# Second parts of the fixed weights on VectorE, and weight sums pipelined over three buffers, in a fused attention, routing and MLP kernel

## The chip, the cores and the metric

One core of a Trainium2 chip. The metric is the device time of one execution in microseconds (us), the median over runs.

## The reference, cut to what matters

```python
# q, k, v: (8, 8, 576, 64); k and v pooled by 8 along the sequence
attn = softmax(scale * q @ k_pool.T) @ v_pool
x = attn.transpose(0, 2, 1, 3).reshape(4608, 512)
# routing: all (token, expert) logits in falling order; a token goes to the first
# of the 8 experts that still has room (capacity 576)
for e in range(8):
    h = np.maximum(x[assigned == e] @ w1[e], 0.0)      # 512 -> 1024
    out[assigned == e] = h @ w2[e]                     # 1024 -> 512
h = np.maximum(out @ w_in, 0.0)                        # 512 -> 2048, fixed weights
result = (h * h) @ w_out                               # 2048 -> 512, fixed weights
```

All inputs and the result are f32.

## The kernel before, in words

After the attention the 4608 tokens are routed, one expert after another, in rounds: a round makes a table `gep` on VectorE (L868), sums it on TensorE (L889), turns the sums on VectorE into counts (`rmd` to `rcd`, L892 to L898), sums again on TensorE (L903) and sets the next bounds on VectorE (`rck` to `rhold`, L905 to L854). Each expert's 576 tokens are then gathered and taken through four layers: the expert's two, the fixed in-layer and the fixed last layer. The text counts them 1 to 4 (or "last").

To keep f32 precision with f16 matmuls, weights and activations are split into two f16 parts, a first part (the rounded value) and a second (the remainder), and each product takes three passes (first by first, first by second, second by first). Expert 0 runs the fixed in-layer plainly (L1266, from `wi`); experts 1 to 7 use a form with seven products of mixed weights (L1403), for which sums and differences of quarters of `w_in` are made once and kept in DRAM as `mixed_weights`. The last layer is L1460, from `wo`.

The program is written out by a Python recorder. The layers of the experts run in the foreground; beside them stand tasks (Python generators: `conv_rest`, `tokens`, `feed`, `routes`, `split_first`, `split_fixed`, `mix_first`) that the recorder advances by estimated engine times: each `yield` names an estimated time from which the task goes on, and `bg.add` gives the order and the engines that it is charged to. What a task records lands on the engines' queues there and then, and every engine works through its queue in order. Small matmuls of the routing so land between the matmuls of the layers.

The tasks that the change touches:

- `split_first` splits `w_in`, eight chunks of 128x1024, in place in `wi`. The first part goes to a side buffer, the second is the chunk minus its first part (`low`, L695), on GpSimd in two halves, into a `gfm` tile of the pool `r_p`; `place` (L699, L700) then copies both into `wi` by DMAs from SP.
- `split_fixed` splits `w_out` into `wo`. The first four chunks go by ACT and GpSimd, the last four, once expert 0's second layer is recorded, by ACT (L779), VectorE (L781) and two DMAs (L782, L783) from two `gfm` tiles.
- `mix_first` first copies the plain quarters to `mixed_weights` (L730, 24 DMAs), then makes the mixed ones in sixteen pieces: load (L740), four sums on GpSimd (L749 to L752), first part on ACT (L755), second on GpSimd (L756), store (L759). Two buffers for the input; one for the parts, in the third slot of `mixb`.
- the gather of the next expert's tokens splits each tile of 128 tokens into `h`, a `gfm` tile, and turns it by a transposing DMA (L1205 to L1208).

The pool `r_p` has two buffers for each name, so a third `gfm` tile waits until the first has been read, here by its DMA. Of `conv_rest`, which decodes the raw weights, the prediction names L661 (VectorE), and of the weight splits of the experts L1106.

## Time and profile before

| what | value |
|---|---|
| median of 3 runs | 1396.54 us (1395.21 to 1402.73) |
| the profiled execution's own time | 1394.52 us |
| its span in the profile | 1392.8 us |
| mean granted TensorE clock | 0.963 |
| PE busy | 1293.1 us (93%) |
| VectorE (DVE) busy | 882.6 us (63%) |
| ScalarE (ACT) busy | 646.7 us (46%) |
| GpSimd (POOL) busy | 443.1 us (32%) |

A busy share is a mean over stages with different limits. PE works nearly all the time, so the places where it stands, and the stretches at a lower clock, are what other engines can take from or give to the time. In the rows below `x24` is the number of instructions in a group, a bracket at the end tells how long the engine stood idle before it and what ended that, and `SPq` is SP issuing DMAs.

### The profile page before, as it was taken

What the parts mean: (1) busy time and instruction counts of PE and PEld (TensorE: products, weight loads), DVE (VectorE), ACT (ScalarE), POOL (GpSimd) and SP (SyncE); (2) the same over time, 40 slices, a digit from 0 to 9 for tenths busy, and PEclk for the clock granted to TensorE, in tenths of its full rate; (3) what the DMA queues carried; (4) which work ended last, traced back from release to release, by engine and by line L of the source; (5) the groups of instructions that cost most, each with busy time, mean ns of one, the idle gap of its engine ahead of it and who ended that gap; (6) DMA issues with size and microseconds to landing.
All of it is one profiled execution on the core that took longest, in us unless ns stands there. A gap on an engine that the chain in (4) does not pass through costs nothing.

```text
span 1392.8 us, 25459 instructions
## 1 busy us (share of the span) xinstructions
PE 1293.1 (93%) x9925; PEld 921.3 (66%) x9925; DVE 882.6 (63%) x2179; ACT 646.7 (46%) x1257; POOL 443.1 (32%) x457
## 2 busy tenths in 40 slices
PE   6999946998896899999999999999999999999997
PEld 5989836775374664776577647764776477657753
DVE  7898886888667786667667765685364325432620
ACT  5777756566523344245524442454345424552520
POOL 4552006247445441134203420342033203310430
PEclk9998957999998899999999999999999999999999
DMA  9877567323632644134703450347035503550500
GB/s 366 351 311 287 176 236 253 99 77 116 172 91 62 216 122 149 42 91 146 211 1 113 136 184 9 91 146 210 1 116 143 174 8 108 150 155 1 153 30 23
DMA packets 133881, 192.39 MB, mean 138 GB/s; under 512 B 58368, under 2 KB 80896, under 8 KB 129024
## 3 DMA queue, kind: packets, MB, share of 16 engines
q1 hardware_dynamic: 122752, 162.45, 36.8%
q0 software_dynamic: 5824, 18.88, 4.0%
q10 hardware_dynamic: 5184, 9.44, 1.8%
q8 instruction: 77, 1.26, 0.4%
q14 instruction: 44, 0.36, 0.1%
HBM read 143.67 MB, written 30.41 MB: 125 GB/s over the span
## 4 chain that ended last, share of the span: by engine, by line
PE 63%; DVE 9%; issue 5%; ACT 3%; POOL 2%; DMA 2%; POOLq 0%; SPq 0%; ACTq 0%; DVEq 0%
PE mm L1266 23%; PE mm L1460 21%; PE mm L1403 18%; DVE e L1106 1%; DVE gep L868 1%; DVE hs L1301 1%; DVE rcd L898 1%; DMA xy<-gfm 0%; DVE xy L1341 0%; DMA hs<-in_w_dram 0%; ACT hs L1300 0%; PE rp L889 0%; POOL mixb L756 0%; ACT qa L1328 0%; ACT xy L1339 0%
## 5 line engine op out<-in xcount | busy, mean ns | idle before, releaser
L1460 PE MATMUL mm<-wo,g 128*128 128x512 f16 x1728 | 382.7, 381 | 0.0
L1266 PEld LDWEIGHTS <-e 128*128 128x128 f16 x3024 | 292.3, 98 | 77.0 <-issue 3.5
L1460 PEld LDWEIGHTS <-g 128*128 128x128 f16 x1728 | 166.6, 98 | 193.9 <-issue 3.0
L1403 PEld LDWEIGHTS <-wi 128*128 128x128 f16 x2352 | 229.9, 98 | 69.5 <-issue 6.0
L1266 PE MATMUL mm<-hs,e 128*128 128x288 f16 x1536 | 193.5, 286 | 0.0
L1266 PE MATMUL mm<-xy,e 128*128 128x288 f16 x1488 | 186.3, 286 | 2.0 <-DVE hs L1301 2.0
L1403 PE MATMUL mm<-wi 128*128 128x288 f16 x1344 | 178.2, 288 | 2.9 <-DVE qa L1425 2.6
L1403 PE MATMUL mm<-xy,wi 128*128 128x288 f16 x1008 | 135.4, 288 | 3.2 <-DMA wi<-mixed_weights 2.2
L1437 POOL TENSOR_TENSOR g<-qa,g 128x576 f16<-128x576 f32 x70 | 101.4, 1459 | 90.3 <-ACT g L1436 90.3
L1471 POOL DMA_INDIRECT out_dram<-qa,idx x32 | 32.2, 1006 | 210.5 <-ACT qa L1468 210.3
L1300 ACT ACTIVATE hs<-mm 128x576 f16<-128x576 f32 x64 | 41.6, 651 | 121.7 <-PE mm L1266 104.9
L1301 DVE SCALAR_TENSOR_TENSOR hs<-mm,hs 128x576 f16<-128x576 f32 x64 | 47.9, 755 | 69.4 <-ACT hs L1300 69.3
L1106 DVE SCALAR_TENSOR_TENSOR e<-hs,e_s,e 128x1024 f16<-128x1024 f32 (+1 forms) x64 | 76.7, 1249 | 22.2 <-ACT e L1105 22.0
L1468 ACT ACTIVATE qa<-mm,uo 128x512 f32<-128x512 f32 x32 | 22.0, 687 | 132.4 <-PE mm L1460 76.2
L453 ACT ACTIVATE es<-sc,mb 128x72 f32<-128x72 f32 x288 | 64.8, 337 | 32.1 <-DVE mb L451 31.9
L1437 POOL TENSOR_TENSOR g<-wi,g 128x576 f16<-128x576 f32 x42 | 58.4, 1390 | 54.7 <-ACT g L1436 54.7
L1425 DVE SCALAR_TENSOR_TENSOR qa<-mm,sg_s,qa 128x576 f32<-128x576 f32 x56 | 45.5, 812 | 44.2 <-ACT qa L1421 39.7
L1105 ACT ACTIVATE e<-hs,e_s 128x1024 f16<-128x1024 f32 (+1 forms) x64 | 65.5, 1084 | 16.6 <-DVE e_s L223 16.6
L1421 ACT ACTIVATE qa<-mm,sg_s 128x576 f32<-128x576 f32 x56 | 41.4, 739 | 64.0 <-PE mm L1403 33.3
L1092 ACT ACTIVATE e<-hs 128x1024 bf16<-128x1024 f32 x60 | 62.7, 1046 | 17.5 <-DMA hs<-in_w_dram 17.2
L475 PE MATMUL po<-vg,et 72*128 72x73 f32 (+1 forms) x608 | 66.3, 272 | 3.3 <-DVE x L501 3.2
L475 PEld LDWEIGHTS po<-vg,et 72*128 72x128 f32 (+1 forms) x608 | 64.1, 188 | 5.5 <-DVE x L501 4.6
(363 smaller groups left out, 1844.3 us busy)
## 6 DMA issues: line engine op xcount, KB each, us to landing
wi<-mixed_weights SPq DMA_DIRECT2D x196, 256.0 KB, 2.7
hs<-in_w_dram SPq DMA_DIRECT2D x60, 512.0 KB, 6.1
tokens_dram<-x ACTq DMA_DIRECT2D x36, 256.0 KB, 5.0
kt<-in_k_dram SPq DMA_DIRECT2D x7, 1152.0 KB, 9.7
vt<-in_v_dram SPq DMA_DIRECT2D x7, 1152.0 KB, 11.8
qt<-in_q_dram SPq DMA_DIRECT2D x7, 1152.0 KB, 7.0
e<-in_win_dram SPq DMA_DIRECT2D x6, 1024.0 KB, 10.3
e<-in_wout_dram SPq DMA_DIRECT2D x4, 1024.0 KB, 5.7
```

The lines of the kernel that those rows point to most:

```text
L453: A.activation(es[i][:, x, :], sc[i, x // 4][:, x % 4, :], AF.Exp, scale=1.0 / 64.0, bias=mb[:, x:x + 1])
L475: T.matmul(p[h // 4][o:o + n, (h % 4) * 73:(h % 4) * 73 + 73], lhsT=et[i][:, h, o:o + n], rhs=vg[b][:, h, :], start=True, stop=True)
L1092: A.activation(dst[:, 0, s2, :].bitcast(BF), staged(st, j)[:, s2, :], AF.Square, accum_out=rm[:, c:c + 1])
L1105: A.activation(dst[:, 0], src, AF.Copy, scale=s)
L1106: V.scalar_tensor_tensor(dst[:, 1], src, s, dst[:, 0], op0=OP.mult, op1=OP.subtract)
L1266: T.matmul(p[:, z, 0:HT], lhsT=lh, rhs=mov(b, c)[:, HALVES[z]], start=c == 0 and a + b == 0, stop=c == kk - 1 and a == 1)
L1300: A.activation(halved(h[:, 0, m]), p, AF.Relu, accum_out=hm[:, m:m + 1])
L1301: V.scalar_tensor_tensor(halved(h[:, 1, m]), p, 0.0, halved(h[:, 0, m]), op0=OP.max, op1=OP.subtract)
L1403: T.matmul(p[:, z, 0:HT], lhsT=w[:, k, u, z], rhs=yq[:, k, v], start=i in (1, 2, 5) and k == 0 and u + v == 0, stop=k == 1 and u == 1, ski ...
L1425: V.scalar_tensor_tensor(q, p, sg["r"], q, op0=OP.mult, op1=OP.add)
L1437: P.tensor_tensor(out=g[:, 1, m:m + 2, gz], in0=q, in1=g[:, 0, m:m + 2, gz], op=OP.subtract)
L1460: T.matmul(o2[c], lhsT=g[:, b, kk, cs], rhs=wo[:, kk // 2, a, kk % 2, :], start=z == 0 and a + b == 0, stop=z == 15 and a == 1)
```

## The change

`split_first`: chunk by chunk one VectorE instruction makes the second part of chunks 0 to 6, where two GpSimd instructions did; chunk 7's stays on GpSimd, in one instruction; the task yields after VectorE's estimated time. `split_fixed`: all eight chunks go by ACT, VectorE and two DMAs, the first of them through `g`, the rest through `gfm`; none by GpSimd. `mix_first`: three input buffers, the parts in `gfm` (two buffers), sums of piece n+1 recorded ahead of the parts of piece n, a pace of 7.0; the task is added ahead of the routing. The gather's `h` lies in `qa`, in three places in turn. The tasks are charged to other engines.

```diff
--- before.py
+++ after.py
@@ -46,6 +46,7 @@
 WARM = 8
 MIDW = 14
 EARLY = 9
+MIXPACE = 7.0
 TICK = 1
 PRE = 1
 DEPTH = 2.0
@@ -691,8 +692,8 @@
         his = [qa[:, 512 * z:512 * z + 512] for z in range(5)] + [mixb[:, 0], mixb[:, 1], hold[:, 3072:3584]]
         his = [h.bitcast(F16) for h in his]
 
-        def low(c, lo, zs):
-            P.tensor_tensor(out=lo[:, zs], in0=words(0, c)[:, zs], in1=his[c][:, zs], op=OP.subtract)
+        def low(c, lo):
+            V.tensor_tensor(out=lo, in0=words(0, c), in1=his[c], op=OP.subtract)
 
         def place(c, lo):
             t = wi[:, c].rearrange("p a b f -> p a (b f)")
@@ -706,17 +707,15 @@
             A.activation(his[c], f, AF.Copy)
             if c == 7:
                 lo = hold[:, 3584:4096].bitcast(F16)
-                for z in range(2):
-                    low(c, lo, slice(z * 512, z * 512 + 512))
+                P.tensor_tensor(out=lo, in0=f, in1=his[c], op=OP.subtract)
                 place(c, lo)
             yield
         for c in range(7):
             lo = r_p.tile([128, 512], F32, name="gfm").bitcast(F16)
-            for z in range(2):
-                low(c, lo, slice(z * 512, z * 512 + 512))
-                bg.work(p=1.1)
-                yield bg.pe + 1.5
+            low(c, lo)
+            bg.work(v=1.25)
             place(c, lo)
+            yield after_v() + 1.0
         done.add(("fixed", 0))
 
     def mix_first():
@@ -731,36 +730,42 @@
                                       in_=wi[:, 2 * k + c, :, 0, gr * 256:gr * 256 + 256])
             yield bg.pe + 1.0
         pieces = [(gr, k, z) for gr in range(4) for k in range(2) for z in range(2)]
-        parts = mixb[:, 2].bitcast(F16).rearrange("p (s a f) -> p s a f", s=4, a=2)
 
         def begin(n):
-            gr, k, z = pieces[n]
-            o = gr * 256 + z * 128
-            for a in range(2):
-                nc.sync.dma_start(out=mixb[:, n % 2].rearrange("p (a b f) -> p a b f", a=2, b=2)[:, a],
-                                  in_=rows4[k, :, a, :, o:o + 128])
-
-        begin(0)
-        begin(1)
-        yield bg.pe + 8.0
+            if n < len(pieces):
+                gr, k, z = pieces[n]
+                o = gr * 256 + z * 128
+                for a in range(2):
+                    nc.sync.dma_start(out=mixb[:, n % 3].rearrange("p (a b f) -> p a b f", a=2, b=2)[:, a],
+                                      in_=rows4[k, :, a, :, o:o + 128])
+
+        def sums(n):
+            if n < len(pieces):
+                a11, a21, a12, a22 = (mixb[:, n % 3, q * 128:q * 128 + 128] for q in range(4))
+                P.tensor_tensor(out=a22, in0=a21, in1=a22, op=OP.add)
+                P.tensor_tensor(out=a21, in0=a11, in1=a21, op=OP.subtract)
+                P.tensor_tensor(out=a11, in0=a22, in1=a11, op=OP.subtract)
+                P.tensor_tensor(out=a12, in0=a12, in1=a11, op=OP.subtract)
+                bg.work(p=2.1)
+
+        for n in range(3):
+            begin(n)
+        yield bg.pe + 8.0, "p"
+        sums(0)
+        first = bg.pe + 2.5
         for n, (gr, k, z) in enumerate(pieces):
-            flat = mixb[:, n % 2].rearrange("p (q f) -> p q f", q=4)
-            a11, a21, a12, a22 = (flat[:, q] for q in range(4))
-            P.tensor_tensor(out=a22, in0=a21, in1=a22, op=OP.add)
-            P.tensor_tensor(out=a21, in0=a11, in1=a21, op=OP.subtract)
-            P.tensor_tensor(out=a11, in0=a22, in1=a11, op=OP.subtract)
-            P.tensor_tensor(out=a12, in0=a12, in1=a11, op=OP.subtract)
-            bg.work(p=2.1)
-            yield bg.p + 2.0
+            yield first + MIXPACE * n, "p"
+            sums(n + 1)
+            parts = r_p.tile([128, 512], F32, name="gfm").bitcast(F16).rearrange("p (s a f) -> p s a f", s=4, a=2)
+            flat = mixb[:, n % 3].rearrange("p (q f) -> p q f", q=4)
             A.activation(parts[:, :, 0], flat, AF.Copy)
             P.tensor_tensor(out=parts[:, :, 1], in0=flat, in1=parts[:, :, 0], op=OP.subtract)
             bg.work(a=0.6, p=1.4)
+            yield bg.p + 0.5, "p"
             o = k * 512 + z * 256
             nc.sync.dma_start(out=mix[gr, 3:7, :, o:o + 256].rearrange("s p f -> p s f"),
                               in_=parts.rearrange("p s a f -> p s (a f)"))
-            yield bg.p
-            if n + 2 < len(pieces):
-                begin(n + 2)
+            begin(n + 3)
         while ("l3", 0) not in done:
             yield later()
         for j in range(WS):
@@ -774,28 +779,19 @@
         for c in range(8):
             f = words(1, c)
             t = wo[:, c].rearrange("p a b f -> p a (b f)")
-            if ("l2", 0) in done:
-                hi = r_p.tile([128, 512], F32, name="gfm").bitcast(F16)
-                A.activation(hi, f, AF.Copy, scale=K["sout"])
-                lo = r_p.tile([128, 512], F32, name="gfm").bitcast(F16)
-                V.scalar_tensor_tensor(lo, f, K["sout"], hi, op0=OP.mult, op1=OP.subtract)
-                nc.sync.dma_start(out=t[:, 0], in_=hi)
-                nc.sync.dma_start(out=t[:, 1], in_=lo)
-                bg.work(a=1.1, v=1.4)
-                yield bg.pe + PACE
-                continue
-            fs = []
+            parts = []
             for z in range(2):
-                zs = slice(z * 512, z * 512 + 512)
                 o = 4096 + 512 * (2 * (c % 2) + z)
-                fs.append(g.rearrange("p a k t -> p (a k t)").bitcast(F32)[:, o:o + 512])
-                A.activation(fs[z], f[:, zs], AF.Copy, scale=K["sout"])
+                p = g.rearrange("p a k t -> p (a k t)").bitcast(F32)[:, o:o + 512]
+                if ("l2", 0) in done:
+                    p = r_p.tile([128, 512], F32, name="gfm")
+                parts.append(p.bitcast(F16))
+            A.activation(parts[0], f, AF.Copy, scale=K["sout"])
+            V.scalar_tensor_tensor(parts[1], f, K["sout"], parts[0], op0=OP.mult, op1=OP.subtract)
             for z in range(2):
-                zs = slice(z * 512, z * 512 + 512)
-                A.activation(t[:, 0, zs], fs[z], AF.Copy)
-                P.tensor_tensor(out=t[:, 1, zs], in0=fs[z], in1=t[:, 0, zs], op=OP.subtract)
-            bg.work(a=2.3)
-            yield bg.pe + 2.5
+                nc.sync.dma_start(out=t[:, z], in_=parts[z])
+            bg.work(a=1.1, v=1.3)
+            yield bg.pe + (PACE if ("l2", 0) in done else 2.5)
         done.add(("fixed", 1))
 
 
@@ -1201,7 +1197,8 @@
         for c in range(NM + 1):
             yield at[c]
             rows = part(c)
-            h = r_p.tile([128, 512], F32, name="gfm").bitcast(F16).rearrange("p (a d) -> p a d", a=2)
+            o = 1024 + 512 * (c % 3)
+            h = qa[:, o:o + 512].bitcast(F16).rearrange("p (a d) -> p a d", a=2)
             A.activation(h[rows, 0], xg[c][rows], AF.Copy, scale=K["sx"][rows])
             V.scalar_tensor_tensor(h[rows, 1], xg[c][rows], K["sx"][rows], h[rows, 0], op0=OP.mult, op1=OP.subtract)
             nc.sync.dma_start_transpose(
@@ -1667,10 +1664,10 @@
     bg.add(conv_rest(), "v")
     bg.add(tokens())
     bg.add(feed())
+    bg.add(mix_first(), "ap")
     bg.add(routes(), "rv")
-    bg.add(conv1, "p")
-    bg.add(conv2, "a")
-    bg.add(mix_first(), "ap")
+    bg.add(conv1, "v")
+    bg.add(conv2, "av")
     for n in range(E):
         mlp(n, None if n else arrive)
         if n + 1 < E:
```

Where the change moves instructions on an engine that waits or is waited for:

VectorE around the end of expert 0's second layer, before (`wo` holds raw chunks of `w_out`, `r...` are tables of the routing):

```order
L892 TENSOR_TENSOR rmd<-rp,blk 120x64
L896 TENSOR_REDUCE rcn<-rmd 120x8
L898 TENSOR_TENSOR rcd<-sel_115,rcn 120x120
L1322 SCALAR_TENSOR_TENSOR xy<-mm_2615,c_s,xy 128x576
L1323 TENSOR_REDUCE ym<-xy 128x1
L232 TENSOR_REDUCE ymx<-ym 128x1
L781 SCALAR_TENSOR_TENSOR gfm<-wo,wout_s,gfm 128x1024
L905 TENSOR_TENSOR rck<-rp,rcb 128x120
L908 TENSOR_REDUCE rpa<-rck 128x8
L923 TENSOR_REDUCE rkm<-rpa 128x1
```

And in the changed program, the last of the three rounds there:

```order
L696 TENSOR_TENSOR gfm<-wi,qa 128x1024
L790 SCALAR_TENSOR_TENSOR gfm<-wo,wout_s,gfm 128x1024
L888 TENSOR_TENSOR rmd<-rp,blk 120x64
L892 TENSOR_REDUCE rcn<-rmd 120x8
L894 TENSOR_TENSOR rcd<-sel_115,rcn 120x120
L696 TENSOR_TENSOR gfm<-wi,mixb 128x1024
L901 TENSOR_TENSOR rck<-rp,rcb 128x120
L904 TENSOR_REDUCE rpa<-rck 128x8
L919 TENSOR_REDUCE rkm<-rpa 128x1
L860 SCALAR_TENSOR_TENSOR rf<-rkm,rba 128x15
```

Before, one 128x1024 pass of a weight split stands in the round; now one or two stand between its steps, three in the rows shown.

PE where expert 0's second layer ends and its third begins, before:

```order
L1266 MATMUL mm_2615<-hs,e_2612 128x288
L1266 LDWEIGHTS e_2612
L1266 MATMUL mm_2615<-hs,e_2612 128x288
L1266 LDWEIGHTS wi
L1266 MATMUL mm_2616<-xy,wi 128x288
```

And in the changed program (`gep`, `rcd` and `onesh` are the routing's; of five L885 the last is shown):

```order
L885 LDWEIGHTS gep
L885 MATMUL rp<-oh,gep 128x64
L899 LDWEIGHTS onesh
L899 MATMUL rp<-rcd,onesh 128x120
L1263 LDWEIGHTS wi
L1263 MATMUL mm_2616<-xy,wi 128x288
```

Before, the two layers follow on one another; now three routing rounds, of which the end of the third is shown, stand between them.

GpSimd at the output of expert 1's second layer (L1334, L1335 and L1354, in the changed program L1331, L1332 and L1351), before:

```order
L1334 TENSOR_TENSOR xy<-qa,xy 128x288
L1335 TENSOR_TENSOR wi<-qa,wi 128x288
L749 TENSOR_TENSOR mixb<-mixb 128x128
L750 TENSOR_TENSOR mixb<-mixb 128x128
L751 TENSOR_TENSOR mixb<-mixb 128x128
L752 TENSOR_TENSOR mixb<-mixb 128x128
L1354 TENSOR_TENSOR wi<-qa,wi 128x2x288
L756 TENSOR_TENSOR mixb<-mixb 128x4x128
L749 TENSOR_TENSOR mixb<-mixb 128x128
L750 TENSOR_TENSOR mixb<-mixb 128x128
L751 TENSOR_TENSOR mixb<-mixb 128x128
L752 TENSOR_TENSOR mixb<-mixb 128x128
```

And in the changed program:

```order
L762 TENSOR_TENSOR gfm<-mixb,gfm 128x4x128
L1331 TENSOR_TENSOR xy<-wi,xy 128x288
L1332 TENSOR_TENSOR wi<-wi 128x288
L762 TENSOR_TENSOR gfm<-mixb,gfm 128x4x128
L1331 TENSOR_TENSOR xy<-qa,xy 128x288
L1332 TENSOR_TENSOR wi<-qa,wi 128x288
L1165 DMA wi<-tokens_dram,idx_5777 128x512 x2
L1165 DMA mixb<-tokens_dram,idx_5777 128x512 x2
L1165 DMA mixb<-tokens_dram,idg_5781 64x512
L1351 TENSOR_TENSOR wi<-qa,wi 128x2x288
```

Before, pieces of the mixed weights stand between and behind the output's steps; now the last one stands between the first two of them.

## Rows read from the trace of the kernel before

**Rows 1.** List of PE's waits: total us, times, longest us.

```profile
PE rp L889 <- DVE gep L868: 15.7, 7, 9.6
...
PE mm L1243 <- DVE xy L1188: 5.4, 1, 5.4
...
PE mm L1266 <- DVE hs L1301: 2.0, 1, 2.0
```

**Rows 2.** Stages: us; busy us of PE, PEld, DVE, ACT, POOL; granted clock, DMA share, GB/s.

```profile
230.00:281.50 51.50, 46.62 (x463) 37.34 (x460) 42.26 (x86) 28.78 (x53) 20.52 (x18) 1.00 0.38 119
281.50:336.60 55.10, 50.80 (x442) 38.51 (x439) 47.72 (x134) 38.36 (x58) 29.93 (x31) 1.00 0.32 106
336.60:389.00 52.40, 45.03 (x221) 20.17 (x219) 34.59 (x86) 24.08 (x36) 25.18 (x31) 0.93 0.55 144
...
438.60:457.20 18.60, 1.39 (x12) 0.69 (x12) 16.63 (x39) 3.76 (x6) 11.86 (x17) 0.64 0.38 107
457.20:558.40 101.20, 98.59 (x632) 59.39 (x633) 73.58 (x165) 45.87 (x68) 35.63 (x33) 0.97 0.54 163
741.10:836.20 95.10, 94.80 (x623) 57.70 (x621) 70.36 (x169) 47.87 (x71) 34.27 (x32) 1.00 0.53 158
```

**Rows 3.** VectorE timeline (start us, us) from 281.8, L661 at 216.53, L661's median.

```profile
L661 DVE SCALAR_TENSOR_TENSOR wo<-e,wo x8: 401/414/5206, 193.1 to 216.5; 128x256 int32<-128x256 int32 x8
...
216.53 5.21 DVE L661 SCALAR_TENSOR_TENSOR wo<-e,wo 128x256 int32<-128x256 int32 x1
...
281.83 0.21 DVE L892 TENSOR_TENSOR rmd<-rp,blk 120x64 f32<-120x64 f32 x1
...
282.58 0.81 DVE L1322 SCALAR_TENSOR_TENSOR xy<-mm,c_s,xy 128x576 f16<-128x576 f32 x1
...
284.26 1.28 DVE L781 SCALAR_TENSOR_TENSOR gfm<-wo,wout_s,gfm 128x1024 f16<-128x1024 f32 x1
285.46 0.27 DVE L905 TENSOR_TENSOR rck<-rp,rcb 128x120 bf16<-128x120 f32 x1
...
287.69 0.17 DVE L854 TENSOR_TENSOR rhold<-rfw,rhold 128x8 f32<-128x8 f32 x1
```

**Rows 4.** GpSimd timeline at 217; the first and the last of sixteen L756.

```profile
216.97 4.48 POOL L695 TENSOR_TENSOR gfm<-wi,qa 128x512 f16<-128x512 f32 x4
...
307.26 1.16 POOL L756 TENSOR_TENSOR mixb<-mixb 128x512 f16<-128x512 f32 x1
...
452.70 1.15 POOL L756 TENSOR_TENSOR mixb<-mixb 128x512 f16<-128x512 f32 x1 [1.07 <-ACT mixb L755]
```

**Rows 5.** PE timeline, stages after expert 0's second layer; brackets: idle before, releaser.

```profile
290.56 3.10 PE L1266 MATMUL mm<-xy,wi 128*128 128x288 f16 x24
...
348.00 6.64 PE L1460 MATMUL mm<-wo,g 128*128 128x512 f16 x30
...
377.33 0.19 PE L236 MATMUL rp<-rsm,onesb 128*128 128x1 bf16 x1 [6.75 <-DVE rsm L232]
...
377.59 8.98 PE L1460 MATMUL mm<-wo,g 128*128 128x512 f16 x30
...
457.21 4.88 PE L1403 MATMUL mm<-xy,wi 128*128 128x288 f16 x24 [2.24 <-DMA wi<-mixed_weights]
```

**Rows 6.** SP timeline with DMA issues; ACT passes that wait for their landing.

```profile
241.42 14.14 SPq L730 DMA_DIRECT2D mixed_weights<-wi  x24
255.60 2.04 SPq L740 DMA_DIRECT2D mixb<-scaled_weights  x4
285.61 0.47 SPq L782 DMA_DIRECT2D wo<-gfm  x1
...
298.50 0.46 SPq L782 DMA_DIRECT2D wo<-gfm  x1
...
288.93 1.15 ACT L779 ACTIVATE gfm<-wo,wout_s 128x1024 f16<-128x1024 f32 x1 [5.45 <-DMA wo<-gfm]
...
300.86 1.15 ACT L779 ACTIVATE gfm<-wo,wout_s 128x1024 f16<-128x1024 f32 x1 [0.73 <-DMA wo<-gfm]
```

## The prediction

> **What bounds the kernel now.** I read the list of PE's waits first, then a table of stages, then the timelines of single engines. PE is the engine that nearly always works; what the change can win are the places where it stands. The list of waits [rows 1] is short: 15.7 us for the routing's `gep` table, of which one wait is 9.6, then single waits of 5.4 and 2.0. The stages [rows 2] say where they lie. Expert 0's second layer ends at 281.5, its third at 336.6, its last at 389.0; layers 1 and 2 of expert 1 take the 49.6 us to 438.6. Then comes a hole: 18.6 us with 1.39 us of PE. Last is the first mixed-weight product with its output, 101.2 us for expert 1 where expert 3, with as many token tiles, takes 95.1.
>
> Each hole has an owner in the timelines. (i) Ahead of expert 0, VectorE's L661 lasts 5.21 us at 216.53, where the median of its eight is 0.41 [rows 3]; beside it GpSimd runs four L695 from 216.97 to 221.45 [rows 4], the second parts of `w_in`. PE waits 5.4 for what VectorE does next, and 2.0 later on [rows 1]. (ii) In the last layer of expert 0 PE waits 6.75 us at 377.33, and the 30 matmuls behind it take 8.98 us, where 30 at 348.00 took 6.64 [rows 5]: gathered tiles pass through the two `gfm` buffers. (iii) The hole at 438.6 ends when the last sums of mixed weights have gone to DRAM and come back: the last L756 starts at 452.70 [rows 4], PE goes on at 457.21 [rows 5].
>
> **The change part by part.**
>
> *A, second parts of w_in off GpSimd.* L661 and the passes behind it go back to their short times: 5.4 + 2.0, and about 0.9 of the 15.7 for `gep`. The three VectorE passes that now lie in layer 2 fit in, as VectorE is busy 42.3 of 51.5 us there [rows 2]. −8.3, so layer 2 ends at 273.2. Least gain 4.6 (third rival).
>
> *B, what the moved passes do ahead of layer 3.* This is the term that I weigh most. In the new order of PE three rounds of expert 1's routing stand ahead of layer 3's first matmul, and between their steps on VectorE lie four `low` passes and the passes of chunks 1 to 3 of `w_out`. Before, the rounds were spread between matmuls of layer 3. So PE waits out this chain. From the end of layer 2: the rest of a round and chunk 0's pass, which begin 24 matmuls (3.1 us) ahead of it and by 2.4 + 1.28 would end 0.6 behind it, but this is the first round, whose form is longer by an estimated 2, so 2.5; the output pass L1322 with the reductions behind it, 282.58 to 284.26, 1.7; three times L892 to L898, 281.83 to the next pass at 282.58 and a little, 0.8 each, 2.5; seven passes at L781's 1.28, 9.0 (an f32 chunk of 128x1024 to f16, as `low` is); two rounds L905 to L854, 285.46 to 287.86, 2.4 each, 4.8 [rows 3]. Work: 20.5. To this come waits for buffers: `low`, first part and second part of a chunk take two `gfm` buffers in turn, and each is free when its placing DMA has landed. From the issue of such a DMA to the ACT pass that waits for its buffer it is 3.3 us once (285.61 to 288.93) and 2.4 once (298.50 to 300.86) [rows 6]; I take 2.9, the middle. Following the ring, chunk 1's and chunk 2's second parts each wait a whole landing for the `low` just ahead, the next two passes 1.3 together: 7.1. Sum 27.6, with PE's hop 28. With 2.4 or 3.3 it is 26 or 29.5; with no wait seen 21.
>
> *C, the clock.* Behind the 18.6 us hole the first 24 matmuls took 4.88 us against 3.10 for 24 at full clock [rows 5]; the granted clock was 0.64 in the hole and 1.00 in layer 3 [rows 2], 1.2 GHz for part of it instead of 2.4. B's gap is longer: +2.
>
> *D, SP's queue in layer 3.* The placing of chunks 5 to 7 now stands behind copies of plain mixed weights, twice twelve, and six loads of mixing input. Before, the 24 copies left SP by 255.6, 14.14 us for all, 0.59 each, and the loads took 0.51 each [rows 6]. Counted from layer 3's start: SP reaches the copies at 3.4, chunk 5 at 10.5, the loads at 18.5, chunk 6 at 21.6; its buffer lands at 24.5; then 1.15 on ACT, 1.28 on VectorE, 0.8 to the routing matmul L899: 28. PE is there after 150 matmuls at 24 in 3.10 [rows 5], 19.4 and some 2 of small ones and waits: 21.5. It waits some 6, and 1 more for routing before that: +7 (1 if SP issues faster, 9 at most).
>
> *E, layer 3 itself.* 55.1 us before [rows 2]; three rounds and their waits have left it: −3.
>
> With A to E layer 3 ends at 336.6 − 8.3 + 28 + 2 + 7 − 3 = 362.3.
>
> *F, gather through `qa`.* Three buffers that no other step shares: the 6.75 and 8.98 − 6.64 = 2.3 go, −9.1. If transposes themselves set the pace, half of it stays.
>
> *G, the hole at 438.6.* The sixteen pieces were 9.7 us apart (307.26 to 452.70 [rows 4]). In GpSimd's new order the last one comes between the first two steps of layer 2's output, where before five came after them. If the pieces keep up, the hole goes: −18.6. GpSimd's 25.2 busy us of 52.4 in expert 0's last layer [rows 2] leave it room.
>
> *H, expert 1's product.* 101.2 falls to expert 3's 95.1: −6.1, as the slow 24 matmuls go and the gather of the next expert comes earlier.
>
> Sum: −8.3 + 28 + 2 + 7 − 3 − 9.1 − 18.6 − 6.1 = −8.1. Against the profiled execution's own 1394.5 us this is 1386.4; the median of the runs stands 2 us above that execution, well inside the uncertainty, so I say 1386.5. What the change wins late it partly pays ahead of layer 3.
>
> **A rule against the rows.** L661 started 0.44 us before the first L695, and ended 0.3 behind the fourth [rows 3, 4]: it lost 4.8 us beside all four, and I count all of it. The Trainium skill, page "SBUF — State Buffer", section "Who interferes with whom", says that VectorE and GpSimd share one port pair as an exclusive lock, and that whoever issues first holds it for the whole instruction, which speaks against A: by it a pass that started first would lose one GpSimd instruction at most, the sum would be 3.7 us higher, and the trace does not look like it.
>
> **The rivals.**
> *Slower, pieces too slow.* If pieces stay 9.7 us apart because their loads, sums and copies wait for one another, the hole comes back. The loads now leave SP some 18 us into layer 3, at 322; with the 8 that the task then asks for (`bg.pe + 8.0`) and an estimated 5 for sums and copy the first piece ends near 335, the last 145.4 later at 480, and with 4.5 us to PE [rows 4, 5] the product starts at 485. Layer 2 of expert 1 would end at 362.3 + 43.3 + 49.6 = 455.2. A hole of 29.7: 1416. It decides from (455.2 − 4.5 − 335)/15 = 7.7 us a piece upward. For it speaks the pace until now; against it the third input buffer, sums that run ahead, and the output that no longer holds the input.
> *Faster, landings hidden.* If the landings don't show, B is 21 and D 1: 1386.4 − 7 − 6 = 1373.5. For it: the shorter of the two landings; against: two buffers for three users.
> *The stall stays.* If the GpSimd passes cost L661 only one of their 1.12 us [rows 4] and the rest of its 5.21 has another cause, A shrinks by 3.7 to 4.6: 1390. For it: L661 started first; against: its end, so close behind the fourth L695. This is what the lock of the Trainium skill's page "SBUF — State Buffer" (same section) would make of it.
> That the change doesn't do what it says is not a case here: seven of the eight subtractions stand on VectorE in its order, and only chunk 7's stays on GpSimd.
>
> **How the numbers follow.** Forecast 0.5, faster rival 0.17, stall 0.15, slower rival 0.18. Half a per cent, 7 us, is about what a measurement can tell from no change: the bounds are 1389.5 and 1403.5. Of the forecast's 0.5 I put 0.34 below the first (B by up to 3 us more still is), 0.14 between, 0.02 above; the faster rival is all below, the stall 0.06 below and 0.09 between, the slower rival above. Faster 0.57, same 0.23, slower 0.20. The range takes the forecast, the faster rival and the stall, 0.82 of the chance, with 3 us below the faster rival and D's and B's upper ends, and half of a late G, above: 1371 to 1405.
>
> **What would show it.** Right: PE stands for about 28 us between layers 2 and 3 of expert 0, from 273 on, with three pairs of L885 and L899 in it; VectorE's L696 and L790 wait there for `wo<-gfm` and `wi<-gfm`; no wait of 5.4 at L1240's matmuls; one wait of some 6 us at L899 in the middle of layer 3; no L237 wait in the last layer; no gap ahead of the first L1400. Wrong: a gap ahead of L1400, L762 more than 7.7 us apart, or less than 21 us ahead of layer 3, which would mean that the chain on VectorE is not what PE waits for.

## The result, and the profile after

The changed kernel takes 1408.96 us (median of 18 runs, 1401.29 to 1417.89) against 1399.21 for the kernel before (18 runs): a ratio of 1.0074, 95% interval 1.0056 to 1.0092. It is slower by some 10 us, where I forecast 10 us faster.

The page of the profiled execution, with the span, PE's share, and PE's busy tenths and granted clock in 40 slices:

```profile
span 1414.3 us, 25439 instructions
...
PE 1306.0 (92%) x9925; PEld 932.7 (66%) x9925; DVE 876.5 (62%) x2190; ACT 641.7 (45%) x1245; POOL 420.0 (30%) x434
...
PE   6999966928889999999999999999999999999997
...
PEclk8799977959999999999999999999999999999999
```

PE's busy time is 13 us more than before for the same number of instructions. Counted from 0, low clock digits stand in slices 0, 1, 5 and 6 and, with a low PE digit, in slice 8. Slice 8 is the stretch that the prediction was about. The others have no part in the result: slices 5 and 6, around the first routing, are low before too (digits 5 and 7), and the attention and the first routing issue the same instructions on every engine in both programs, but for chunk 7's second part, one GpSimd instruction instead of two. The first matmul of expert 0 (L1240) starts at 229.97 here and at 218.32 before by what the clock does ahead of it (last section). From that matmul to the end it is 1184.3 us here and 1174.5 before: 9.8 more, which is what the medians say (9.75). So I count from there.

The stages, as in [rows 2] (us; busy us of PE, PEld, DVE, ACT, POOL; granted clock, DMA share, GB/s): to the end of expert 0's layer 2, the wait, layer 3, the last layer, layers 1 and 2 of expert 1, its product with the output. Ahead of them the first stage of the kernel before, counted from the same matmul:

```profile
218.32:281.50 63.18, 52.93 (x524) 43.40 (x523) 50.83 (x94) 33.51 (x61) 26.52 (x23) 0.94 0.45 143
```

```profile
229.97:283.00 53.03, 50.44 (x523) 41.23 (x522) 43.21 (x93) 25.32 (x46) 0.00 (x0) 1.00 0.16 60
283.00:312.72 29.72, 1.60 (x19) 0.86 (x17) 17.85 (x39) 5.22 (x5) 0.00 (x0) 0.58 0.33 124
312.72:380.20 67.48, 56.63 (x435) 41.90 (x436) 43.48 (x131) 38.63 (x59) 32.41 (x36) 0.86 0.49 153
380.20:429.60 49.40, 45.08 (x219) 20.10 (x217) 32.08 (x66) 24.16 (x34) 36.70 (x47) 0.93 0.67 181
429.60:482.60 53.00, 50.31 (x429) 39.56 (x428) 38.57 (x116) 15.54 (x33) 26.96 (x37) 0.97 0.38 113
482.60:577.70 95.10, 94.81 (x624) 57.77 (x622) 67.05 (x154) 47.57 (x71) 28.33 (x27) 1.00 0.52 146
```

Look at the second row: 29.72 us with 1.60 of PE, a stretch that did not exist. Layer 3 takes 67.5 (55.1 before), at a clock of 0.86. Layers 1 and 2 of expert 1 end at 482.60, where its product starts: the hole of 18.6 is gone.

PE's list of waits has new heads; where 15.7 for `gep` led [rows 1], now 27.4 for `rcd` do:

```profile
PE rp L899 <- DVE rcd L894: 27.4, 6, 6.7
PE rp L885 <- DVE gep L864: 11.4, 2, 7.1
...
PE rp L993 <- DVE roq L986: 7.8, 4, 3.7
```

PE's timeline from layer 2's end, first of the waits for the three rounds (five in all, 3.60, 7.08, 6.53, 4.35 and 6.56), then the slow places of layer 3, the one of the last layer, and one of expert 1's layer 2:

```profile
286.78 0.23 PE L899 MATMUL rp<-rcd,onesh 120*128 120x120 f16 x1 [3.60 <-DVE rcd L894]
294.09 0.42 PE L885 MATMUL rp<-oh,gep 128*128 128x64 bf16 x5 [7.08 <-DVE gep L864]
...
312.65 0.28 PE L899 MATMUL rp<-rcd,onesh 120*128 120x120 f16 x1 [6.56 <-DVE rcd L894]
312.72 6.63 PE L1263 MATMUL mm<-xy,wi 128*128 128x288 f16 x30
...
341.97 0.28 PE L899 MATMUL rp<-rcd,onesh 120*128 120x120 f16 x1 [6.68 <-DVE rcd L894]
342.05 4.91 PE L1263 MATMUL mm<-xy,wi 128*128 128x288 f16 x24
...
359.17 0.30 PE L993 MATMUL rp<-rmv,roq 128*128 128x72 f16 x4 [2.41 <-DVE roq L986]
...
361.21 3.07 PE L1263 MATMUL mm<-xy,wi 128*128 128x288 f16 x12
...
364.36 4.00 PE L1263 MATMUL mm<-xy,wi 128*128 128x288 f16 x24
...
419.09 0.26 PE L899 MATMUL rp<-rcd,onesh 120*128 120x120 f16 x1 [3.74 <-DVE rcd L894]
419.15 6.57 PE L1457 MATMUL mm<-wo,g 128*128 128x512 f16 x18
...
458.13 0.23 PE L241 MATMUL rp<-identb,hmx 128*128 128x128 bf16 x1 [2.69 <-DVE hmx L233]
```

VectorE in the wait. The bracket of 3.1 is the landing of a `low` that a second part of `w_out` waits for (there are two such); the other two are later `low` passes that wait for `wo<-gfm`:

```profile
286.64 1.22 DVE L696 TENSOR_TENSOR gfm<-wi,qa 128x1024 f16<-128x1024 f32 x1
291.00 1.28 DVE L790 SCALAR_TENSOR_TENSOR gfm<-wo,wout_s,gfm 128x1024 f16<-128x1024 f32 x1 [3.13 <-DMA wi<-gfm]
...
302.63 1.23 DVE L696 TENSOR_TENSOR gfm<-wi,mixb 128x1024 f16<-128x1024 f32 x1 [1.65 <-DMA wo<-gfm]
...
310.61 1.23 DVE L696 TENSOR_TENSOR gfm<-wi,mixb 128x1024 f16<-128x1024 f32 x1 [2.38 <-DMA wo<-gfm]
```

### The profile page after: what moved, and what is told of

It is laid out like the page before. It is cut to its first block, busy times and chain, and to the rows that moved or that the text cites. A ratio compares the mean times of both kernels' runs of the same rounds, so it can differ in the third digit from the quotient of the medians.

```text
span 1414.3 us, 25439 instructions
## 1 busy us (share of the span) xinstructions
PE 1306.0 (92%) x9925; PEld 932.7 (66%) x9925; DVE 876.5 (62%) x2190; ACT 641.7 (45%) x1245; POOL 420.0 (30%) x434
## 4 chain that ended last, share of the span: by engine, by line
PE 61%; DVE 4%; issue 3%; ACT 1%; POOL 1%; POOLq 0%
PE mm L1263 21%; PE mm L1457 21%; PE mm L1400 18%; DVE hs L1298 0%; DVE gep L864 0%; PE rp L885 0%; DVE qa L1422 0%; DVE e L1102 0%; POOL out_dram L1468 0%; POOL g L1434 0%; ACT hs L1297 0%; DVE qa L1427 0%; ACT e L1101 0%; DVE rf L860 0%; DVE rpa L904 0%
## 5 line engine op out<-in xcount | busy, mean ns | idle before, releaser
L1434 POOL TENSOR_TENSOR g<-qa,g 128x576 f16<-128x576 f32 x70 | 100.5, 1445 | 95.1 <-ACT g L1433 95.1
L454 ACT ACTIVATE es<-sc,mb 128x72 f32<-128x72 f32 x288 | 64.7, 337 | 33.8 <-DVE mb L452 33.6
L1434 POOL TENSOR_TENSOR g<-wi,g 128x576 f16<-128x576 f32 x42 | 57.9, 1378 | 52.3 <-ACT g L1433 52.3
L476 PE MATMUL po<-vg,et 72*128 72x73 f32 (+1 forms) x608 | 70.8, 282 | 2.4 <-DVE x L502 2.3
L476 PEld LDWEIGHTS po<-vg,et 72*128 72x128 f32 (+1 forms) x608 | 68.6, 199 | 4.9 <-DVE x L502 3.8
```

What stands on the lines that cost most here:

```text
L454: A.activation(es[i][:, x, :], sc[i, x // 4][:, x % 4, :], AF.Exp, scale=1.0 / 64.0, bias=mb[:, x:x + 1])
L476: T.matmul(p[h // 4][o:o + n, (h % 4) * 73:(h % 4) * 73 + 73], lhsT=et[i][:, h, o:o + n], rhs=vg[b][:, h, :], start=True, stop=True)
L1434: P.tensor_tensor(out=g[:, 1, m:m + 2, gz], in0=q, in1=g[:, 0, m:m + 2, gz], op=OP.subtract)
```

## The experiments

My theory after the result: PE stands ahead of layer 3 for a chain on VectorE that is made long by three users of two `gfm` buffers (the ring: `low` and the two parts of `w_out`), and layer 3 is long by SP's queue and the clock behind each wait; against it, that the loss is spread over later stages that the other parts made. All kernels stage by stage, in us, from PE's timelines, counted from the first matmul of expert 0 (layers 1 and 2 of expert 0; the wait; layer 3; last layer; layers 1 and 2 of expert 1; hole; product with output):

| kernel | ratio to before (95%) | 1, 2 | wait | 3 | last | e1: 1, 2 | hole | product |
|---|---|---|---|---|---|---|---|---|
| before | 1 | 63.2 | 0 | 55.1 | 52.4 | 49.6 | 18.6 | 101.2 |
| changed | 1.0074 (1.0056 to 1.0092) | 53.0 | 29.7 | 67.5 | 49.4 | 53.0 | 0 | 95.1 |
| `after_again` | 1.0052 (1.0024 to 1.0080) | 55.4 | 29.7 | 69.0 | 48.9 | 53.0 | 0 | 95.1 |
| `early` | 0.9997 (0.9967 to 1.0027) | 52.9 | 0 | 72.3 | 52.3 | 56.2 | 0 | 99.6 |
| `pool_low` | 0.9927 (0.9899 to 0.9955) | 60.9 | 0 | 69.0 | 52.0 | 49.8 | 0 | 96.5 |
| `low_alone` | 1.0200 (1.0147 to 1.0254) | 53.0 | 33.6 | 64.0 | 51.4 | 53.8 | 18.0 | 102.2 |
| `own_place` | 0.9824 (0.9779 to 0.9870) | 63.4 | 0 | 59.2 | 51.5 | 49.8 | 0 | 96.2 |
| `mix_gather` | 0.9830 (0.9788 to 0.9873) | 63.2 | 0 | 61.6 | 54.6 | 49.6 | 0 | 96.1 |
| `gather_alone` | 0.9948 (0.9916 to 0.9980) | 63.7 | 0 | 55.1 | 48.1 | 49.5 | 18.7 | 101.2 |
| `low_buffer` | 0.9959 (0.9928 to 0.9991) | 53.4 | 19.3 | 67.8 | 48.1 | 52.8 | 0 | 95.1 |
| `hold_rounds` | 1.0081 (1.0039 to 1.0122) | 53.3 | in 3 | 98.6 | 50.9 | 49.9 | 0 | 96.2 |
| `copies_late` | 1.0106 (1.0042 to 1.0171) | 53.5 | 29.7 | 55.0 | 45.4 | 53.0 | 20.3 | 100.7 |
| `early_own` | 0.9873 (0.9792 to 0.9954) | 53.0 | 0 | 54.0 | 53.9 | 56.5 | 0 | 99.5 |
| `own_hold` | 0.9905 (0.9872 to 0.9937) | 53.3 | in 3 | 77.5 | 51.0 | 49.8 | 0 | 96.0 |

**`after_again`**: the changed kernel, for a second trace.

> The changed kernel unchanged, for a second trace. Theory: from the first matmul of expert 0's layer 1 on the stages repeat to within 1 us (29.7 ahead of layer 3, no hole ahead of expert 1's first product); what differed by 11.7 us ahead of that, in the attention, is the granted clock there and does not repeat: 1409 by the median. Rival: the 11.7 us repeat, and are part of what the change costs.

1407.8 us. The wait is 29.7 again, the hole is away again; layers 1 and 2 and layer 3 differ by 2.4 and 1.5, more than the 1 us that I allowed. The late start (230.27) came again as well, so this run does not tell what makes it; `copies_late`, with the same instructions up to layer 3, starts at 218.56, and all the traces together tell it (last section).

**`low_alone`**: of the change only `split_first`.

```diff
-            P.tensor_tensor(out=lo[:, zs], in0=words(0, c)[:, zs], in1=his[c][:, zs], op=OP.subtract)
+            V.tensor_tensor(out=lo, in0=words(0, c), in1=his[c], op=OP.subtract)
...
+            yield after_v() + 1.0
...
-    bg.add(conv1, "p")
+    bg.add(conv1, "v")
```

> The kernel before with only the second parts of w_in on VectorE. Three routing rounds and four of the passes stand ahead of layer 3, without passes of w_out between them. Theory (chain): the early gain of 10, then a wait ahead of layer 3 of about 17 (work of 15, hardly a wait for a landing, as only the passes use the two buffers) and 2 to 3 of slow clock, and the hole ahead of expert 1's first product grows from 18.6, as the pieces can only start after the last pass: 1405 to 1435. Rival (spread): with the other parts not made, the time is below that of the kernel before.

1429.9 us, inside the range, by another split: the early gain of 10 and the wait are there, but the wait is 33.6 and not 17. I had left out that the last four chunks of `w_out` stand in it here too, with their own use of the two buffers. The hole did not grow (18.0), but begins later.

**`pool_low`**: all of the change but that part.

```diff
-            V.tensor_tensor(out=lo, in0=words(0, c), in1=his[c], op=OP.subtract)
+            P.tensor_tensor(out=lo[:, zs], in0=words(0, c)[:, zs], in1=his[c][:, zs], op=OP.subtract)
...
-            yield bg.p + 0.5, "p"
...
-    bg.add(conv1, "v")
+    bg.add(conv1, "p")
```

> The changed kernel without its first part: the second parts of w_in are made on GpSimd in halves as before, all else as changed (the store of a mixed piece is recorded at once). Theory (chain): no wait ahead of layer 3, the early waits of 5.4 and 2.0 come back, the hole ahead of expert 1's first product stays away: 1409 - 30 - 6 + 10, about 1383 (1375 to 1390). Rival (spread): the other parts cost what the first part was blamed for, and the time stays above 1395.

1388.9 us, faster than before by 0.7%. The wait is gone, the hole stays away. But layer 3 takes 69.0 with no wait ahead of it, so it is long for a reason of its own. ACT and VectorE in it:

```profile
300.36 0.63 ACT L763 ACTIVATE gfm<-mixb 128x512 f16<-128x512 f32 x1 [6.20 <-DMA wo<-gfm]
...
309.71 0.63 ACT L763 ACTIVATE gfm<-mixb 128x512 f16<-128x512 f32 x1 [3.85 <-DMA wo<-gfm]
...
314.20 1.28 DVE L791 SCALAR_TENSOR_TENSOR gfm<-wo,wout_s,gfm 128x1024 f16<-128x1024 f32 x1 [5.96 <-DMA mixed_weights<-gfm]
```

A mixed piece waits for `wo<-gfm`, and a second part of `w_out` for `mixed_weights<-gfm`: two users of one ring stand in each other's landings, and the routing's passes stand behind them.

**`own_place`**: `pool_low` with `w_out`'s parts in `g`.

```diff
-                o = 4096 + 512 * (2 * (c % 2) + z)
+                o = (3840, 8960)[z] + 512 * (c % 2)
                 p = g.rearrange("p a k t -> p (a k t)").bitcast(F32)[:, o:o + 512]
-                if ("l2", 0) in done:
-                    p = r_p.tile([128, 512], F32, name="gfm")
```

> The version pool_low (second parts of w_in on GpSimd, all else as changed) with the two parts of every chunk of w_out in g, in the places that layer 3 writes last, so that the two gfm buffers serve the mixed pieces alone. In pool_low layer 3 took 69.0 us, before 55.1. Theory (one ring, several users): w_out's parts and the mixed pieces wait for each other's landing, VectorE stands in those waits and the routing behind it; with a place of their own layer 3 takes 55 to 58: 1389 - 12, about 1377. Rival: layer 3 is long because SP carries 24 copies, loads and stores more, or because GpSimd's sums slow VectorE; then it stays at 66 or more and the time at 1386 to 1391.

1373.5 us (4 runs), 1.8% faster than before, and the best of all. Layer 3, first in `pool_low`, then here:

```profile
276.40:345.40 69.00, 53.60 (x441) 39.86 (x439) 49.45 (x131) 41.89 (x63) 36.99 (x40) 0.95 0.40 130
```

```profile
277.20:336.50 59.30, 50.90 (x440) 38.51 (x439) 51.44 (x131) 42.16 (x63) 39.83 (x40) 1.00 0.47 152
```

Layer 3 falls by 9.8 to 59.2, a little above the 55 to 58 expected. SP carries the same copies, loads and stores and GpSimd the same sums, so the shared ring was the cause.

**`low_buffer`**: the changed kernel with `low` outside the ring.

```diff
-            lo = r_p.tile([128, 512], F32, name="gfm").bitcast(F16)
+            lo = mixb[:, 2].bitcast(F16)
```

> The changed kernel with the second parts of w_in in the idle third slot of mixb instead of gfm, nothing else. Theory (chain with landings): the two full landings of 3.1 us that the parts of w_out wait for behind them, and the 1.7 and 2.4 that the next two wait, go from the wait ahead of layer 3: 29.7 falls to 20 to 23, and the time by 7 to 10, to 1400. Rival: the landings only fill time that the rounds need anyway; the wait stays above 27 and the time at 1408.

1392.4 us. The wait falls from 29.7 to 19.3, just below the 20 to 23 expected. VectorE's brackets in it are 0.3 and 0.7 instead of 3.1, 3.1, 1.7, 0.8 and 2.4:

```profile
283.97 1.28 DVE L790 SCALAR_TENSOR_TENSOR gfm<-wo,wout_s,gfm 128x1024 f16<-128x1024 f32 x1 [0.30 <-ACT gfm L789]
...
286.71 1.23 DVE L696 TENSOR_TENSOR mixb<-wi,mixb 128x1024 f16<-128x1024 f32 x1 [0.70 <-DMA wi<-mixb]
```

So some 10 of the wait were landings, and the 18.3 without brackets are the work that I had put at 20.5. The median falls by 16, more than the wait does; from the first matmul of expert 0 to the end, trace against trace, it is 12.8 to 16.1.

**`hold_rounds`**: no rounds ahead of layer 3.

```diff
-            yield bg.p + 0.5, "p"
...
     def wait(*events):
         while not done.issuperset(events):
-            bg.tick(0.5)
+            bg.tick(0.5, hold="r")
```

> The changed kernel with the routing held back while the program waits for the fixed weights, so that no round stands ahead of layer 3 (the store of a mixed piece is recorded at once). Theory (landings through two buffers): the passes and their landings take nearly as long alone; each pair of low and second part of w_out needs a pass, a landing of 3.1 and a pass, and every third tile waits for the one before, so PE's wait ahead of the first quarter or so of layer 3 is still 22 to 27, though for the placed chunks and no longer for the routing, and the rounds are paid again in layer 3: 1400 to 1412. Rival (work of the rounds): they are the chain, the wait falls by 10 or more to below 20 and the time to 1395 or less.

1410.4 us. PE starts layer 3 and waits 13.5 and 15.3 in its first matmuls, now for the placed chunks themselves:

```profile
271.29 0.97 PE L1262 MATMUL mm<-xy,wi 128*128 128x288 f16 x6
...
285.94 1.09 PE L1262 MATMUL mm<-xy,wi 128*128 128x288 f16 x3 [13.54 <-DMA wi<-qa]
302.37 3.96 PE L1262 MATMUL mm<-xy,wi 128*128 128x288 f16 x15 [15.34 <-DMA wi<-mixb]
```

28.9 in all, above my 22 to 27: the passes and landings take as long without the rounds. The rounds did not make the wait; they stood in it. Without the two waits layer 3 takes 69.7, so nothing is won.

**`own_hold`**: this with `low` in `mixb` and `w_out`'s parts in `g` (the diffs of `low_buffer` and `own_place` on `hold_rounds`).

> The changed kernel with all three: w_in's second parts in mixb's third slot, w_out's parts in g, rounds held back while the program waits for the fixed weights. Theory: what is left ahead of layer 3 is four passes of 1.2 and landings of 3.1 through one buffer, 12 to 18, and layer 3 takes 60 or less: 1375 to 1388. Rival: the wait stays near 19 as in low_buffer.

1385.7 us, in the range; PE waits 9.8 and 7.6, 17.4, inside 12 to 18. Layer 3 without them is 60.1.

**`copies_late`**: term D, by putting off the copies and the sums of mixed weights.

```diff
-        while ("fixed", 0) not in done:
+        while not done.issuperset([("fixed", 0), ("fixed", 1)]):
             yield later()
```

> The changed kernel with the 24 copies and the sums of mixed weights only after all chunks of w_out are recorded, so that SP places chunks 5 to 7 without copies and loads ahead of them. Theory (term D): the wait of 6.7 us at L899 in the middle of layer 3 and the slow 24 matmuls behind it go, layer 3 falls from 67 to 58 to 60; the pieces start some 15 us later, so a hole of 15 to 35 comes back ahead of expert 1's first product: 1410 to 1430. Rival: the wait stays, as the two buffers and not SP's queue hold the last chunk's second part; layer 3 stays at 65 or more.

1411.0 us. SP places chunks 4 to 7 in one go and then copies; the wait of 6.7 is 0.78, the 24 matmuls behind it take 3.11 instead of 4.91, and the routing's later waits shrink too:

```profile
305.33 19.41 SPq L792 DMA_DIRECT2D wo<-gfm  x8
324.79 6.47 SPq L729 DMA_DIRECT2D mixed_weights<-wi  x12
...
324.90 0.23 PE L899 MATMUL rp<-rcd,onesh 120*128 120x120 f16 x1 [0.78 <-DVE rcd L894]
324.96 3.11 PE L1263 MATMUL mm<-xy,wi 128*128 128x288 f16 x24
```

Layer 3 takes 55.0, not 58 to 60: all that it had lost comes back. That is more than D: the edit also takes the mixed pieces out of layer 3 (the first L761 is at 371.41, in the last layer), so it does not separate SP's queue from them. The wait and the 24 matmuls behind it give 5.9 and 1.8. The routing's passes L964 to L986 take 6.2 us here, where they took 9.2 with pieces on GpSimd beside them; PE's waits for `roq` and the slow matmuls behind them give most of the rest. The later pieces cost a hole of 20.3.

**`early`** and **`early_own`**: `split_first` first in the list, so that all seven passes lie ahead of layer 2's end; `early_own` has `w_out`'s parts in `g` too (the diff of `own_place`).

```diff
+    bg.add(conv1, "v")
     bg.add(conv_rest(), "v")
...
-    bg.add(conv1, "v")
...
-            yield bg.p + 0.5, "p"
```

> The changed kernel with split_first listed ahead of the decoding of the raw weights, so that all seven second parts of w_in stand on VectorE ahead of the end of expert 0's second layer and no routing round stands between layers 2 and 3 (the store of a mixed piece is also recorded at once). Theory (chain): PE's wait of 29.7 us between layers 2 and 3 goes, and with it most of the slow stretches behind it; the early gain of 10 shrinks by 0 to 5, since 8.5 us of VectorE passes move into a busy stretch. 1409 - 30 - 5 + 3, about 1377 (1370 to 1390). Rival (spread): the loss sits in later waits that the new traffic makes (6.7 in layer 3, 3.7 in the last layer, 2.7 in layer 2 of expert 1); then at most the 29.7 go and other waits take their place: 1390 to 1400.

> The version early (second parts of w_in on VectorE ahead of layer 2's end, no rounds ahead of layer 3) with w_out's parts in g as in own_place. Theory: layer 3 falls from 72 to 60, the early gain of 10 stays, and the slower layers 1 and 2 of expert 1 (56 against 50) stay too: 1401 - 13, about 1388 (1378 to 1392), so GpSimd remains the better place for w_in's second parts (own_place 1373.5). Rival: with the ring freed VectorE is the better place, and the time falls below 1372.

1401.2 and 1376.5 us. `early` missed: the wait of 29.7 is gone and the early gain kept, but layer 3 takes 72.3 and layers 1 and 2 of expert 1 56.2. I had not counted that the ring's users meet in layer 3 wherever the passes of `w_in` go. With the ring freed layer 3 takes 54.0 (60 expected), and the time is just below the range; the slower layers of expert 1 stayed, as said. That VectorE is the better place is not shown: `own_place`, with GpSimd, is 3 us faster, but with four runs each the two intervals overlap, so neither is the reverse.

**`mix_gather`** and **`gather_alone`**: the other two parts on the kernel before, the pipelined sums and the gather through `qa`, and the latter alone.

```diff
-            h = r_p.tile([128, 512], F32, name="gfm").bitcast(F16).rearrange("p (a d) -> p a d", a=2)
+            o = 1024 + 512 * (c % 3)
+            h = qa[:, o:o + 512].bitcast(F16).rearrange("p (a d) -> p a d", a=2)
```

> The kernel before with the pipelined sums of mixed weights and the gather through qa, both fixed weights split as before (the store of a mixed piece is recorded at once). Theory: the hole of 18.6 us ahead of expert 1's first product goes, its product takes 96 instead of 101, the last layer of expert 0 about 49; layer 3 grows by some 10, as the last four chunks of w_out share the gfm buffers with the pieces: 1398 - 18.6 - 5 - 3 + 10, about 1382. Rival: the hole went only because the changed kernel started its pieces elsewhere; then it stays at 10 or more and the time above 1392.

> The kernel before with only the gather's h in three places of qa. Theory: the transposing DMAs set the pace, so the last layer of expert 0 gains only the 3 us that it gained in the changed kernel: 1395. Rival: the shared buffers were the whole of it, the last layer falls by 9 as I forecast and the changed kernel lost 6 there for another cause: 1389.

1376.5 (4 runs) and 1392.6 us. The hole's 18.6 and 5 of the product are the pipelined sums'; layer 3's +6.5 (10 expected) I put down to their share in the ring, as in `pool_low`. Alone the gather brings 4.3 of the last layer, nearer to theory (3) than to rival (9); a wait of 3.1 is left of the 6.75 [rows 5]:

```profile
374.45 0.18 PE L236 MATMUL rp<-rsm,onesb 128*128 128x1 bf16 x1 [3.12 <-DVE rsm L232]
```

This gain does not hold everywhere. In `mix_gather` I expected 49 for the last layer; it takes 54.6, more than before, with waits of 5.1 and 2.1. `pool_low` and `own_place`, with the same gather, take 52.0 and 51.5, with waits of 5.9 and 5.5 for `rsm`. What decides it was not tried.

## Why the prediction was wrong, step by step

- **A, right and a little more**: layer 2 ends 10.1 and 7.8 earlier in the two traces of the change, 8.3 forecast. L661 (now L662) takes 0.42 with no GpSimd pass beside it; in the four other versions that left these passes on GpSimd its longest takes 4.96 to 5.35:

```profile
226.12 0.42 DVE L662 SCALAR_TENSOR_TENSOR wo<-e,wo 128x256 int32<-128x256 int32 x1
```

  The rival in which most of the stall stays is out by this: it left a gain of 4.6, and every trace with these passes on VectorE shows 7.8 to 10.3. It is the rival that the lock of the Trainium skill's page "SBUF — State Buffer", section "Who interferes with whom", would give; the traces here do not bear it out. What each single GpSimd instruction held was not tried.
- **B, right, in part by luck**: 28 forecast, 29.7 and 29.7 measured. Two errors offset each other: the waits were 11.1, with landings of 3.1 where I took 2.9 and 4.8 for three later waits (1.65, 0.78, 2.38) where I took 1.3 for two, so 4 more than my 7.1; the work was some 2 less than my 20.5 (18.3 in `low_buffer`).
- **C, D and E, too small by 6**: +6 together, +12.4 and +13.9 measured. The failing step is C, "B's gap is longer: +2": it prices the low clock behind that one gap, and the other waits of layer 3 stand in my sum without it. The matmuls were slow behind three waits. The 30 behind B's gap took 6.63 where 30 take 3.83 at full clock, +2.8; the 24 behind D's wait 4.91 where 3.10 are usual, +1.8; the 12 and 24 behind the waits for `roq` 3.07 and 4.00 where 1.64 and 3.10 are usual, +2.3. That is 6.9 (6.5 in `after_again`). D's own wait came as forecast, 6.68 us at 341.97 and 0.31 ahead of it, 7.0 in all, with SP's queue as said:

```profile
317.56 6.49 SPq L729 DMA_DIRECT2D mixed_weights<-wi  x12
...
325.32 6.66 SPq L729 DMA_DIRECT2D mixed_weights<-wi  x12
...
336.04 6.29 SPq L792 DMA_DIRECT2D wo<-gfm  x4
...
338.70 1.15 ACT L789 ACTIVATE gfm<-wo,wout_s 128x1024 f16<-128x1024 f32 x1 [7.22 <-DMA wo<-gfm]
```

  The waits for `roq` (2.41 and 1.45, before 0.54 and 1.45) I had put at nothing, +1.9. VectorE has no wait there; its passes take longer, the last two 3.58 us against 1.42 in `copies_late`, and mixed pieces run on GpSimd beside them. That the pieces are the cause was not tried by itself:

```profile
357.29 3.58 DVE L986 TENSOR_TENSOR roq<-rqi,row 128x576 bf16<-128x576 int32 x2
```

  What is left for E, by difference, is some −3.4, where I had −3.
- **F, too large by 6**: −9.1 forecast, −3.0 and −3.5 measured. Alone it is −4.3 (`gather_alone`). The sentence that failed is "Three buffers that no other step shares: the 6.75 and 8.98 − 6.64 = 2.3 go"; the case named behind it, in which the transposes set the pace and half of the gain stays, is nearer. With five tiles and three buffers ACT waits 3.22 for one to be turned, VectorE's passes, among them the weight splits of the next expert, come behind that, and PE waits 3.74 at 419.09. The clock's part, my 2.3, did not go at all: the 18 matmuls behind that wait take 6.57, where 18 took 4.05. In `copies_late` the same wait is 2.95 and the 18 behind it take 4.05, and the last layer falls by 7.0; so how much of F comes depends on the clock too:

```profile
412.03 0.72 ACT L1202 ACTIVATE qa<-wi,x_s 128x512 f16<-128x512 f32 x1 [3.22 <-DMA xy<-qa]
```

- **Priced at nothing, +3.4**: layers 1 and 2 of expert 1. With the routing of expert 2 shifted, two L986 stand on VectorE ahead of the reduction that PE waits for, 2.69 at 458.13:

```profile
454.96 2.37 DVE L986 TENSOR_TENSOR roq<-rqi,row 128x576 bf16<-128x576 int32 x2
```

  Where that wait is 0.2 to 0.7, as before, these layers take 49.5 to 49.9. (The 56 of `early` and `early_own` come with another wait there, 5.0 and 4.7 for `rcd`.)
- **G and H, right**: −18.6 and −6.1 forecast and measured. The slower rival, pieces too slow, did not happen: 16 pieces from 345.65 to 467.67 are 8.1 us apart, above the 7.7 that I called decisive, but layer 3 was so much longer that they still came in time.
- The sum: −10.1 + 29.7 + 12.4 − 3.0 + 3.4 − 18.6 − 6.1 + 2.2 (all after expert 1, not taken apart) = +9.9, against −8.1. The loss ahead of layer 3 came by the mechanism that I forecast, and the gains A, G and H came too. The sign was lost by three terms: C, 2 where the slow matmuls cost 6.9; F, −9.1 where −3.0 came; and expert 1, at nothing where it cost 3.4. I gave 0.20 to slower, nearly all of it for a mechanism that did not occur.

## What to carry to other kernels

A ring of two buffers with several users can cost up to a whole landing at a change of user (0.8 to 3.1 us here), and whatever stands behind the waiting pass on its engine waits too; give the users places of their own before moving work between engines (here one line took 13 to 16 us off the changed kernel). Price each wait of PE with what follows it: in the changed kernel the next matmuls took 1.8 to 2.8 us more behind waits of 2.4 to 6.7 us, and nothing more behind one of 2.95 in `copies_late`. A part that helps alone (the pipelined sums and the gather, 1.7%) can hide in a change whose first part costs more.

## What was not expected of the hardware

The same instructions of the attention took different times by the granted clock. At 21 us PE waits some 2 us for ACT; behind it 16 matmuls L475 (now L476) take 1.90 us before and 3.52 and 3.53 in two others, of which the changed kernel stays slow until 51 us and `copies_late` only until 31. Before, changed, `copies_late`:

```profile
21.06 1.07 PE L461 MATMUL pt<-ident,es 128*72 128x128 f32 x8 [1.90 <-ACT vg L420]
21.96 1.90 PE L475 MATMUL po<-vg,et 72*128 72x73 f32 x16
```

```profile
21.08 1.59 PE L462 MATMUL pt<-ident,es 128*72 128x128 f32 x8 [1.93 <-ACT vg L421]
22.47 3.52 PE L476 MATMUL po<-vg,et 72*128 72x73 f32 x16
```

```profile
21.22 1.92 PE L462 MATMUL pt<-ident,es 128*72 128x128 f32 x8 [2.07 <-ACT vg L421]
22.93 3.53 PE L476 MATMUL po<-vg,et 72*128 72x73 f32 x16
...
30.23 2.33 PE L476 MATMUL po<-vg,et 72*128 72x73 f32 x16
```

The waits are 1.90, 1.93 and 2.07 us, and both levels are seen behind them: 16 matmuls in 1.90 at 2.4 GHz, in 3.53 at 1.2. Expert 0's first matmul starts between 213.9 (`own_place`) and 230.3 (`after_again`), and over the fourteen traces the later it starts the lower is the mean granted clock up to it, from 0.88 to 0.81; late starts come with `early`, `low_alone` and `own_hold` as well as with the changed kernel. The changed kernel's 18 runs spread over 17 us. One profiled execution of each program can so differ by more than a change is worth, at a place where the programs are the same.
